# A two-pass planner, one load sequence with few loads on ScalarE, and equal units in a fused delta-rule and MLP kernel

## The chip, the cores and the metric

One core of a Trainium2 chip. The metric is the device time of one execution in microseconds, median over the runs of a kernel. Executions of this kernel have a faster and a slower state: runs over 1.5% above the fastest of the same kernel are called slow and are left out of ratios. Chips differ too: the same kernel before has a median of 415.7 us on the first chip and of 421.6 to 423.4 us on four others, so kernels are compared through the runs of the kernel before on the same chip.

## The reference, cut to what matters

```python
# attention part: batch 4, 8 heads, 768 steps, head size 48
k_n = k / (norm(k) + 1e-6)
for t in range(S):
    y[t]  = g[t] * (q[t] @ state)
    v_old = state.T @ k_n[t]
    state = state + beta[t] * outer(k_n[t], v[t] - v_old)
# then, on the 3072 x 384 result
h = x @ w_in                                        # 384 -> 2048
a = where(h >= 1, h, where(h <= -1, 0, (h + 1)**2 / 4))
out = a @ w_out                                     # 2048 -> 384
```

## The kernel before

The recurrence is cut into 24 steps of 32 tokens, all 32 (batch, head) pairs at once. The work is a list of tasks; a planner (a small simulation that runs while the kernel is built) decides the order of each engine, and the instructions are emitted in that order. In the first profile each engine's computing instructions stand in that order, line by line: all 9,792 matmuls of TensorE, and all computing instructions of ScalarE, VectorE and GpSimd.

Per step, TensorE has the chain kp, up, su (64, 32 and 64 small matmuls) and as fillers the gram group of a later step (64) and the output y (96). For every group of 4 steps there is an inverse of 32x32 triangular blocks, which costs 2 times 128 small matmuls and a serial run of small VectorE or GpSimd instructions. Each small matmul has its own weight load (the first profile counts 9,792 matmuls and 9,792 weight loads in all).

```python
def f_su():                                   # state update, 64 matmuls of 32x32 by 48
    for par in range(2):
        for j in range(J):
            for h4 in range(4):
                nc.tensor.matmul(sps[32*h4:32*h4+32, par, D*j:D*j+D], kq..., u16..., ...)
...
def pe_dur(n): return n * 0.0076              # the plan's time of n small matmuls
```

The MLP works on units of 2 or 4 steps. An "in" task is one PSUM bank of `x @ w_in` (three matmuls of 512 columns, or six of 256), then ScalarE, ScalarE or GpSimd, and VectorE form the activation `gt`; four "out" tasks of four matmuls make 128 rows of the output.

```python
UNITS = [2, 2, 4, 4, 4, 4, 2, 2]
TAIL = 20.0                                   # us of large products left for the end
```

Loads of q, k, v, g come in pieces of 48 KB. Whichever of the sync engine and ScalarE the plan finds free first issues them:

```python
if eng == "SP" and kind == "load":
    alt = [("ACT", dur, lambda ...: nc.scalar.dma_start(out=tile_, in_=src))]
```

Of the kernel before, what the change touches and what calls it, by code (L numbers as in the profile page):

```python
# [10 lines left out]
ALU = mybir.AluOpType  # L11
# [44 lines left out]
class Task:  # L56
    __slots__ = ("opts", "D", "reads", "writes", "deps", "left", "users", "ready", "start", "end", "eng", "fn", "kind", "name", "n", "after", "after_cost", "elems")
# [8 lines left out]
class Plan:  # L66
# [28 lines left out]
    def run(self, nbank, pol):  # L95
        engs = ["PE", "ACT", "DVE", "POOL", "SP"]
        free = {e: 0.0 for e in engs}
        cand = {e: [] for e in engs}
        banks = [[0.0, None] for _ in range(nbank)]
        dma_free = 0.0  # L100
        order = []

        def release(t):
            for e, d, f in t.opts:
                cand[e].append(t)

        for t in self.tasks:
            if t.left == 0:
                release(t)

        def bank_for(t, at):
            for v in t.writes:
                if v.psum and v.bank is None:
                    if pol.psum_full(v.psum):
                        return INF
                    b = min((b[0] for b in banks if b[1] is None), default=INF)
                    return b
            return 0.0

        def dur_of(t, e):  # L120
            for x, d, f in t.opts:
                if x == e:
                    return d, f

        def pick(e):
            c = cand[e]
            if not c:
                return None
            t0 = max(free[e], min(t.ready for t in c))
            if e == "PE":  # L130
                return pol.pick(c, free[e], bank_for)
            hot = [t for t in c if t.kind == "chain"]
            best = None
            late = lambda t: t.kind == "load" and e == "ACT" and t.D > -35.5
            av = sorted((t for t in c if t.ready <= t0 + 1e-9), key=lambda t: (t.kind != "chain", late(t), t.D, t.n))
            for t in av:
                d, _ = dur_of(t, e)
                if t.kind != "chain" and any(h.ready > t0 and t0 + d > h.ready + 0.25 for h in hot):
                    continue
                return t, t0  # L140
            nxt = min((t.ready for t in c if t.ready > t0 + 1e-9), default=None)
            if nxt is None:
                return None
            h = min((t for t in c if t.ready > t0 + 1e-9), key=lambda t: t.ready)
            return h, h.ready

        left = len(self.tasks)
        while left:
            best = None
            for e in engs:  # L150
                p = pick(e)
                if p is not None and (best is None or p[1] < best[1] - 1e-9):
                    best = (p[0], p[1], e)
            if best is None:
                raise RuntimeError("the plan is stuck: " + str([(e, [t.name for t in cand[e]][:8]) for e in engs]) + str([(t.name, [d.name for d in t.deps if d.start is None][:4]) for t in self.tasks if t.start is None and t.left][:12]))
            t, s, e = best
            d, fn = dur_of(t, e)
            if e == "PE":
                d = d + pol.switch(t)
            t.start, t.eng, t.fn = s, e, fn  # L160
            free[e] = s + d
            t.end = s + d
            if t.kind in ("load", "store"):
                dma_free = max(dma_free, s + d + 0.8) + t.after_cost
                t.end = dma_free + 1.2
            for x, _, _ in t.opts:
                cand[x].remove(t)
            for v in t.writes:
                if v.psum and v.bank is None:
                    i = min((i for i in range(nbank) if banks[i][1] is None), key=lambda i: banks[i][0])  # L170
                    v.bank = i
                    banks[i][1] = v
                    pol.psum_take(v.psum)
            for v in list(t.reads) + list(t.writes):
                if v.psum and v.bank is not None and banks[v.bank][1] is v:
                    if all(x.start is not None for x in v.r) and all(x.start is not None for x in v.w):
                        banks[v.bank] = [max(x.end for x in v.r) + LAT, None]
                        pol.psum_give(v.psum)
            pol.done(t)
            order.append(t)  # L180
            left -= 1
            for u in t.users:
                u.left -= 1
                lat = LAT if e != u.opts[0][0] else 0.0
                u.ready = max(u.ready, t.end + lat)
                if u.left == 0:
                    release(u)
        self.span = max(t.end for t in self.tasks)
        return sorted(order, key=lambda t: (t.start, t.n))


class Policy:


    def __init__(self, nstep, units, tail):
        self.nstep, self.tail = nstep, tail
        self.step = 0
        self.inphase = False
        self.mode = None
        self.mlp_left = 0.0  # L200
        self.quota = 0.0
        self.cnt = {"c": 0, "m": 0, "o": 0}
        self.last_mlp = None
        self.lim = {"c": 3, "m": 3, "o": 1}
        self.step_of_mlp = 0
# [16 lines left out]
    def pick(self, c, free, bank_for):  # L222
        def rdy(t):
            return max(t.ready, bank_for(t, free), free)
        chain = [t for t in c if t.kind == "chain"]
# [41 lines left out]
    def done(self, t):  # L267
        if t.eng != "PE":
            return
        if t.kind == "chain":  # L270
# [4 lines left out]
        elif t.kind in ("in", "out"):  # L275
# [4 lines left out]
            if t.kind == "in":  # L280
                for u in t.elems:
                    u.D = self.step + 0.3
# [3 lines left out]
def kernel(  # L286
# [98 lines left out]
    def load_task(D, tile_, src, names, cost, val, eng="SP", dur=0.46, kind="load"):  # L385
        def fn(tile_=tile_, src=src):
            ENG[eng].dma_start(out=tile_, in_=src)
        alt = []
        if eng == "SP" and kind == "load":
            alt = [("ACT", dur, lambda tile_=tile_, src=src: nc.scalar.dma_start(out=tile_, in_=src))]  # L390
        t = P.add(eng, dur, D, fn, [], [val], kind, names, alt=alt)
# [3 lines left out]
    vin = {}  # L395

    def loads(p):
        gi = p // 2
        for nm, src, R, D0 in (("k", k, R_k, 4 * gi - 14), ("q", q, R_q, 4 * gi - 13.9), ("v", v, R_v, 4 * gi - 9), ("g", g, R_g, 4 * gi - 7)):
            val, t = R.new(f"{nm}{p}")  # L400
            vin[nm, p] = (val, t)
            for c in range(2):
                s = 2 * p + c
                for h4 in range(4):
                    a = bass.AP(tensor=src.tensor, offset=src.offset + h4 * S * D + s * C * D, ap=[[D, C], [HS, J], [1, D]])
                    if gi == 0:
                        DD = -40 + {("k", 0): 0, ("k", 1): 1, ("q", 0): 2, ("q", 1): 3, ("v", 0): 4, ("v", 1): 5, ("g", 0): 6, ("g", 1): 7}[nm, p]
                    else:
                        DD = D0 + (p % 2) * 1.0
                    load_task(DD, t[32 * h4:32 * h4 + 32, c], a, f"ld{nm}{p}", 0.285, val)  # L410

    vbeta = Val("beta")
    for st in range(4):
        for h4 in range(4):
            a = bass.AP(tensor=beta.tensor, offset=beta.offset + h4 * S + st * C, ap=[[4 * S, J], [GS * C, NG], [1, C]])
            load_task(-37, braw[32 * h4 + 8 * st:32 * h4 + 8 * st + 8], a, "ldb", 0.05, vbeta, "POOL", 0.45)
# [37 lines left out]
    def prep_pair(p):  # L454
# [7 lines left out]
        P.add("ACT", acost(768), D0, lambda: act("ACT", sqt[:], flat(kt_), AF.Square), [kv], [sq], "", f"ksq{p}")  # L462
# [10 lines left out]
              [kv, v3, nv, vz_kq[a.slot]], [vk, a], "", f"kh{p}")  # L473
# [264 lines left out]


    def w_in_task(a, half, r0, ap_rows):  # L740
        src = bass.AP(tensor=moe_w_in.tensor, offset=moe_w_in.offset + r0[0] * DFF + half * 1024, ap=ap_rows + [[1, 1024]])
        dst = win[r0[1]:r0[1] + r0[2], a, half * 1024:half * 1024 + 1024]
        load_task(-26.6 + 0.05 * half, dst, src, f"win{a}", 1.5 * r0[2] / 128, vwin[half], "POOL", 0.6)

    for half in range(2):
        w_in_task(0, half, (0, 0, 128), [[D * DFF, 4], [DFF, 32]])
        w_in_task(2, half, (4 * D + 16, 0, 128), [[D * DFF, 4], [DFF, 32]])
        for h4 in range(4):
            w_in_task(1, half, (h4 * D + 32, 32 * h4, 32), [[160 * DFF, 2], [DFF, 16]])
    for qd in range(4):  # L750
        src = bass.AP(tensor=moe_w_out.tensor, offset=moe_w_out.offset + qd * 4 * 128 * DM, ap=[[DM, 128], [128 * DM, 4], [1, DM]])
        load_task(-21 + 0.1 * qd, wout[:, 4 * qd:4 * qd + 4, :], src, "wout", 2.2, vwout, "POOL", 0.7)


    for p in range(NSTEP // 2):
        loads(p)
    for gi in range(NG):
# [14 lines left out]
    pol.mlp_left = sum(t.opts[0][1] for t in P.tasks if t.kind in ("in", "out"))  # L772
    order = P.run(NB, pol)
# [7 lines left out]
UNITS = [2, 2, 4, 4, 4, 4, 2, 2]  # L781
TAIL = 20.0
DEBUG = []
# [28 lines left out]
```

## Time and profile before

| | us |
|---|---|
| median, first chip | 415.7 |
| profiled execution (slow) | 424.8 |
| its first su (state update of step 0) | 68.5 |
| its last su (step 22) | 375.1 |
| its last matmul | 412.9 |

How to read it: three regions, cut at those instants. The start fills the buffers and makes the inverse of group 0; the middle is the recurrence with the MLP between; the tail is MLP alone, then the last stores. The profile's lines are shown in the prediction. PE is TensorE, DVE VectorE, ACT ScalarE, POOL GpSimd, SP the sync engine; a trailing q marks an engine's DMA issues. A bracket at the end of a line is how long the engine stood idle before it, and what ended that.

### The profile page before, as it was taken

The page shows a single profiled execution, that of the slowest core. Times are in us where ns is not written, and L with a number is a line of the kernel's source. Part 1 is how long each engine was busy: PE and PEld are TensorE (multiplying, and loading weights), DVE is VectorE, ACT ScalarE, POOL GpSimd, SP SyncE. Part 2 cuts the span into 40 slices and gives each one's busy share as a digit, 9 for nine tenths or more (in the row PEclk, how much of TensorE's full clock was granted, in tenths as well). Part 3 has the DMA queues.
Part 4 walks back from the last instruction along what each step waited for, and adds up shares of the span by engine and source line. Part 5 has one row for each costly group of instructions (what it writes and reads, how often), then busy time and mean ns, then how long its engine had stood idle before and what let it go on. Part 6 is the DMA issues. An engine that isn't in the chain of part 4 may idle for free.

```text
span 424.8 us, 21311 instructions
## 1 busy us (share of the span) xinstructions
PE 261.1 (61%) x9792; PEld 167.7 (39%) x9792; DVE 170.4 (40%) x318; ACT 167.5 (39%) x301; POOL 140.3 (33%) x261
## 2 busy tenths in 40 slices
PE   0030014577876644367578669689867888989980
PEld 0030014455654324334344434445443553546750
DVE  2230824334784225234553535335423313555500
ACT  0500004143782123036353435256544424768920
POOL 8681001035496341045513563058400001011100
PEclk9999999995995665568685759579886986999996
DMA  7899976432334245443313224014011100001101
GB/s 128 130 128 175 149 143 115 75 66 45 66 56 83 62 94 101 95 72 50 60 27 65 46 43 94 5 31 106 13 31 40 42 22 22 22 5 39 39 30 44
DMA packets 114793, 28.23 MB, mean 66 GB/s; under 512 B 108688, under 2 KB 113936, under 8 KB 114704
## 3 DMA queue, kind: packets, MB, share of 16 engines
q1 hardware_dynamic: 77600, 18.16, 22.2%
q10 hardware_dynamic: 30192, 5.46, 7.5%
q0 software_dynamic: 6912, 3.26, 5.5%
q8 instruction: 76, 1.25, 1.2%
q14 instruction: 13, 0.11, 0.1%
HBM read 25.26 MB, written 4.72 MB: 71 GB/s over the span
## 4 chain that ended last, share of the span: by engine, by line
PE 54%; DMA 19%; issue 17%; DVE 3%; POOL 2%; ACT 2%; SPq 1%; ACTq 1%
PE bank L699 18%; PE bank L725 16%; DMA rk<-in_k_dram 5%; DMA rg<-in_g_dram 5%; PE sps L638 4%; DMA rq<-in_q_dram 4%; DMA rv<-in_v_dram 3%; PE bank L654 3%; PE bank L494 3%; PE bank L611 3%; PE bank L627 2%; DMA out_dram<-ot 2%; PE bank L575 2%; PE bank L660 2%; PE bank L562 1%
## 5 line engine op out<-in xcount | busy, mean ns | idle before, releaser
L699 PE MATMUL bank<-xt,win 128*128 128x512 f16 (+1 forms) x384 | 94.1, 381 | 5.9 <-issue 4.7
L725 PE MATMUL bank<-wout,gt 128*128 128x384 f16 x384 | 87.5, 366 | 0.6 <-DVE gt L708 0.6
L708 DVE SCALAR_TENSOR_TENSOR gt<-bank,r 128x512 f16<-128x512 f32 x96 | 63.4, 681 | 47.1 <-ACT r L373 32.6
L373 ACT ACTIVATE rl<-bank 128x512 f32<-128x512 f32 x96 | 56.4, 596 | 58.3 <-PE bank L699 55.7
L705 POOL TENSOR_TENSOR r<-rl 128x512 f32<-128x512 f32 x25 | 26.0, 1041 | 116.6 <-ACT rl L373 96.1
L725 PEld LDWEIGHTS <-gt 128*128 128x128 f16 x384 | 38.9, 107 | 34.1 <-issue 14.9
L699 PEld LDWEIGHTS <-win 128*128 128x128 f16 x384 | 39.2, 109 | 32.0 <-issue 15.6
L472 POOL TENSOR_TENSOR kq<-rk,nn 128x768 f16<-128x768 f32 x12 | 17.7, 1478 | 85.0 <-DMA rv<-in_v_dram 38.2
L494 PE MATMUL bank<-kt 24*32 24x64 f16 x1536 | 22.3, 217 | 37.5 <-DVE nn L467 21.5
L373 ACT ACTIVATE r<-rl 128x512 f32<-128x512 f32 x71 | 43.9, 629 | 1.6
L665 DVE TENSOR_TENSOR y<-bank,rg 128x384 f16<-128x384 f32 x24 | 13.3, 556 | 67.6 <-PE bank L660 48.6
L494 PEld LDWEIGHTS <-kt 24*32 24x32 f16 x1536 | 19.0, 109 | 41.0 <-DVE nn L467 21.5
L616 DVE TENSOR_TENSOR rr<-rv,bank 128x384 f16<-128x384 f32 x23 | 12.7, 552 | 44.7 <-PE bank L611 44.6
L562 PE MATMUL bank<-d,ab 16*32 16x16 f16 x768 | 7.8, 173 | 34.8 <-DVE d L552 25.7
L638 PE MATMUL sps<-u,kq 32*32 32x48 f16 x1472 | 18.6, 194 | 16.5 <-ACT u L373 8.6
L373 ACT ACTIVATE u<-bank 128x384 f16<-128x384 f32 x24 | 11.8, 490 | 42.5 <-PE bank L627 34.6
L373 ACT ACTIVATE s<-sps 128x768 f16<-128x768 f32 x23 | 18.6, 809 | 20.2 <-PE sps L638 19.8
L535 POOL TENSOR_TENSOR xx<-xx,tm 128x28 f32<-128x28 f32 (+6 forms) x70 | 24.3, 347 | 5.2
L654 PE MATMUL bank<-s,kt 24*32 24x48 f16 x1472 | 19.4, 198 | 10.3 <-issue 10.3
L638 PEld LDWEIGHTS <-kq 32*32 32x32 f16 x1472 | 15.4, 98 | 25.5 <-issue 24.8
L532 POOL TENSOR_TENSOR tm<-xx 128x28 f32<-128x28 f32 (+6 forms) x70 | 23.5, 335 | 4.9
L373 ACT ACTIVATE ab<-bank 128x256 f16<-128x256 f32 x24 | 9.1, 382 | 39.6 <-DMA rg<-in_g_dram 15.0
(54 smaller groups left out, 288.7 us busy)
## 6 DMA issues: line engine op xcount, KB each, us to landing
out_dram<-ot SPq DMA_DIRECT2D x24, 192.0 KB, 1.8
rg<-in_g_dram SPq DMA_DIRECT2D x71, 48.0 KB, 2.7
rq<-in_q_dram SPq DMA_DIRECT2D x69, 48.0 KB, 2.6
rk<-in_k_dram SPq DMA_DIRECT2D x67, 48.0 KB, 3.0
rv<-in_v_dram SPq DMA_DIRECT2D x66, 48.0 KB, 2.7
wout<-in_moe_w_out_dram POOLq DMA_DIRECT2D x4, 384.0 KB, 11.1
rv<-in_v_dram ACTq DMA_DIRECT2D x30, 48.0 KB, 2.4
rk<-in_k_dram ACTq DMA_DIRECT2D x29, 48.0 KB, 2.8
```

The source lines that it names most:

```text
L373: nc.scalar.activation(out=out, in_=in_, func=func, **kw)
L472: P.add("POOL", 1.5, D0 + 0.3, lambda: nc.gpsimd.tensor_tensor(out=kqf[:, :, 0, 0:D], in0=flat(kt_), in1=_ap(nt, [[1, 2 * J], [0, D]], 3 * ...
L494: nc.tensor.matmul(b[32 * h4:32 * h4 + 32, 64 * j:64 * j + 64], _apr(kt, 32 * h4, 24, [[2, 32]], j * 128 + par), _apr(kt, 32 * h4, 24, [[2 ...
L532: P.add(sub, d, D0 + 0.1 * jj, lambda jj=jj, n=n, tm=tm: seng.tensor_tensor(out=_ap(tm, [[n * jj, 2], [jj, n], [1, jj]]), in0=_ap(x, [[256 ...
L535: P.add(sub, d, D0 + 0.1 * jj, lambda jj=jj, n=n, tm=tm: seng.tensor_tensor(out=_ap(x, [[256, 2], [16, n], [1, jj]], (jj + 1) * 16), in0=_ ...
L638: nc.tensor.matmul(sps[32 * h4:32 * h4 + 32, par, D * j:D * j + D], _apr(kqt, 32 * h4, 32, [[2, 32]], (c * J + j) * 128 + par), u16[32 * h ...
L654: nc.tensor.matmul(b[32 * h4:32 * h4 + 32, D * j:D * j + D], _apr(kt, 32 * h4, 24, [[2, 32]], j * 128 + 64 + par), s16[32 * h4:32 * h4 + 2 ...
L665: P.add("DVE", dcost(384), s + 0.5, lambda: nc.vector.tensor_tensor(out=y16[:], in0=_ap(bk(yp), [[D, J], [1, D]]), in1=gt_[:, c], op=ALU.m ...
L699: nc.tensor.matmul(b[:, x * nt:x * nt + nt], win[:, kt_, m * 128:m * 128 + 128], xt[:, kt_ * nt:kt_ * nt + nt], start=(kt_ == 0), stop=(kt ...
L705: t2 = P.add("POOL", pcost(512), 0, lambda: nc.gpsimd.tensor_tensor(out=r2[:], in0=rl[:], in1=rl[:], op=ALU.mult), [rv], [r2v], "elem", f" ...
L708: t3 = P.add("DVE", dcost(512), 0, lambda: nc.vector.scalar_tensor_tensor(out=gt[:], in0=bk(hp)[:], scalar=1.0, in1=r2[:], op0=ALU.max, op ...
L725: nc.tensor.matmul(b[:, 0:DM], gt[:, o:o + 128], wout[:, m, :], start=(m == 0), stop=(m == NM - 1))
```

## The change

Its intent: plan TensorE's order first as if the other engines were free, then plan all engines with deadlines that follow from TensorE's times; fix one sequence of loads, with only twelve of them on ScalarE; hold the weights back until the first groups are loaded; make all MLP units two steps long. The core of the diff:

```diff
-        if eng == "SP" and kind == "load":
-            alt = [("ACT", dur, lambda ...: nc.scalar.dma_start(out=tile_, in_=src))]
-        t = P.add(eng, dur, D, fn, [], [val], kind, names, alt=alt)
+        t = P.add(eng, dur, D, fn, [], [val], kind, names)
...
+    FIRST = "k0 k1 q0 q1 k2 q2 k3 q3 v0 v1 g0 g1 v2 k4 q4 k5 q5 v3 g2 g3".split()
+                    on_act = (nm == "k" and p < 2 or nm == "q" and p < 1) and h4 % 2 == 1
+                    eng = "ACT" if on_act else "POOL" if nm + str(p) in POOL_LOADS else "SP"
...  # beta: 16 loads become 4 loads and two VectorE transposes
...  # squares and scaling of k0, k1 may also run on VectorE
+            t = P.add("POOL", 0.65, D, fn, [vin[gate][0]], vals, "load", f"win{a}")   # waits for v0 or v1
+            t = P.add("POOL", 0.7, ..., fo, [vin["v", 3][0]], [vwout], "load", "wout")
...
-    order = P.run(NB, pol)
+    order = P.plan(NB, pol, PASSES)
+    def plan(self, nbank, pol, passes):
+        order = self.run(nbank, pol, ("ACT", "DVE", "POOL"))     # these engines free
+        for i in range(passes):
+            self.deadlines(SLOW)
+            pol.order = {t: n for n, t in enumerate(x for x in order if x.eng == "PE")}
+            order = self.run(nbank, pol)                          # the best pass is kept
...
-UNITS = [2, 2, 4, 4, 4, 4, 2, 2]
+UNITS = [2] * 12
```

## The prediction

> **What bounds the kernel now.** I read the page first (busy shares, slices, chain), then windows cut at the chain's own steps, the list of waits of TensorE, and TensorE's timeline. The page:
>
> ```profile
> PE 261.1 (61%) x9792; PEld 167.7 (39%) x9792; DVE 170.4 (40%) x318; ACT 167.5 (39%) x301; POOL 140.3 (33%) x261
> PE   0030014577876644367578669689867888989980
> PEclk9999999995995665568685759579886986999996
> DMA  7899976432334245443313224014011100001101
> PE 54%; DMA 19%; issue 17%; DVE 3%; POOL 2%; ACT 2%; SPq 1%; ACTq 1%
> ```
>
> TensorE, the busiest engine, is almost unused in the first six of 40 slices (64 us), while DMA is at its fullest; the chain of waits is 54% TensorE, and 17% "issue", waiting for nothing that the profile shows. So there are three regions: a start, the recurrence, a tail. I cut them at the first state update (su of step 0, 68.5 us), the last (375.1) and the last matmul (412.9):
>
> ```profile
> core 0: us, PE busy (x) PEld busy (x) DVE busy (x) ACT busy (x) POOL busy (x), PEclk, DMA share, GB/s
> 0.00:68.50 68.50, 6.88 (x548) 6.15 (x551) 23.98 (x65) 10.23 (x17) 28.91 (x48) 1.00 0.92 142
> 68.50:375.10 306.60, 218.92 (x8681) 137.11 (x8684) 130.25 (x229) 131.30 (x240) 106.22 (x208) 0.77 0.28 55
> 375.10:412.90 37.80, 35.28 (x575) 24.45 (x574) 16.14 (x25) 25.44 (x44) 5.20 (x5) 1.00 0.08 29
> ```
>
> The start: on ScalarE's timeline
>
> ```profile
> 21.63 5.01 ACTq L390 DMA_DIRECT2D rg<-in_g_dram  x4
> 36.49 0.38 ACT L373 ACTIVATE ab<-bank 128x256 f16<-128x256 f32 x1 [9.42 <-DMA rg<-in_g_dram]
> 58.07 5.72 ACTq L390 DMA_DIRECT2D rv<-in_v_dram  x8
> 63.97 0.84 ACT L373 ACTIVATE ksq<-rk 128x768 f32<-128x768 f32 x1 [20.79 <-DMA rv<-in_v_dram]
> 64.72 0.58 ACT L373 ACTIVATE p<-bank 128x512 f16<-128x512 f32 x1
> ```
>
> ScalarE stands behind its own load issues. The gram matmuls of group 0 were done by 30.4 us, but the last eviction `ab` ran at 43; the first matmul of the inverse ran at 56.1 to 57.3, but its eviction `p` at 64.7. About 12 and 7 us of the start are ScalarE blocked by loads that are needed much later.
>
> The recurrence: TensorE's timeline from 160 us
>
> ```profile
> 166.96 0.54 PE L638 MATMUL sps<-u,kq 32*32 32x48 f16 x35 [0.31 <-issue]
> 167.30 1.06 PE L494 MATMUL bank<-kt 24*32 24x64 f16 x64
> 168.14 0.50 PE L654 MATMUL bank<-s,kt 24*32 24x48 f16 x29
> 170.97 0.54 PE L654 MATMUL bank<-s,kt 24*32 24x48 f16 x35 [2.33 <-issue]
> 171.30 0.52 PE L660 MATMUL bank<-u,ms 32*32 32x48 f16 x32
> 171.62 0.69 PE L562 MATMUL bank<-d,ab 16*32 16x16 f16 x61
> 174.97 0.68 PE L562 MATMUL bank<-d,ab 16*32 16x16 f16 x67 [2.65 <-issue]
> ```
>
> The engine stops in the middle of groups that need no semaphore there. From stop to stop it is 35+64+29 = 128 matmuls, with their weight loads 256 instructions; the same holds for nearly all stops of the trace, and never less than about 3.73 us pass between two of them 256 apart. The queue kind "instruction" has 76 packets of 16 KB, and 19,594 instructions are 76.5 times 256. So TensorE is fed by instruction blocks, and one block costs at least 3.73 us. Waits of TensorE on other engines in this region sum to under 20 us: I call it bound by TensorE, by instruction blocks where matmuls are small, by the clock where they are large.
>
> The large matmuls (input product, L699) are very unevenly spread:
>
> ```profile
> 95.70:132.80 37.10, 10.86 (x72) 7.40 (x72) 0.79 0.34 60
> 132.80:187.30 54.50, 4.11 (x9) 1.01 (x9) 0.56 0.44 84
> 187.30:245.20 57.90, 17.27 (x46) 4.64 (x45) 0.74 0.30 52
> 375.10:424.80 49.70, 14.60 (x103) 9.81 (x102) 0.93 0.09 33
> ```
>
> 72 of 384 run while step 4 waits for group 1, 9 in steps 4 to 7, 103 after the last update. With 120 of the 384 output matmuls, 29% of the feed-forward part is left over for the tail.
>
> [...]
>
> **The change, part by part.**
>
> *Loads in one sequence, few on ScalarE.* ScalarE keeps 12 loads (half of k0, k1, q0). In the trace one tensor of one pair (8 loads, 384 KB) takes about 2.7 us in the chain (2.52 to 3.19). So k0, k1, q0, q1 are in by about 14 us, as now. From there with the durations of the trace: ksq 0.84, reduce 0.95, root, add and reciprocal 0.6, kq 1.5, two transposes of 0.7, two gram groups 1.9: about 7 us for each pair, pair 1 by 20 us (now 30.4). Then `ab` 0.4, and from the first transpose `at` to the `d` and `zz` transposes the trace has 43.2 to 56.9, 13.7 us. Then 1.2 + 0.6 + 1.2 + 0.7 for the two inverse products and evictions, up and u 1.0. That sums to 39; with waits between engines I take 42 for the first su instead of 68.5: minus 26.5. Beta comes in 4 transfers instead of 16 (571 ns each on GpSimd: about 7 us of GpSimd less), but 24 loads of k2, v0, v1 and the weights go to GpSimd; at 0.64 us they take 15 us, beside the inverse of group 0 on VectorE.
>
> *Weights wait for v0, v1 and v3.* At 142 GB/s the first two pairs (3.1 MB) take 22 us undisturbed; now the weights start at 13.5 us among them. The weights then land by about 45 and 75 us, an estimate; the first input product is possible when y0 and y1 are done, about 55 us. This costs nothing if the output product has enough else ahead of it.
>
> *Units of 2 throughout.* Sixteen products of 3 matmuls over 512 columns become eight of 6 over 256, in four units, each twice: 384 input matmuls become 576. With weight loads 384 instructions more, 1.5 blocks, at most 6 us. Columns are the same: the page of groups and the timeline have 0.65 us for six of 256 as for three of 512 at full clock. The gain is that input products become ready every 2 steps, so steps 4 to 7 are not left without.
>
> *Planner.* It has no model of instruction blocks or of the half clock, so it can't aim at either. It should spread large matmuls by quota and leave 20 us of them for the tail.
>
> *Sum, in the profiled run's time.* The middle now: 17,365 instructions, 67.8 blocks, in 306.6 us: 4.52 us each. The stretches differ: 187 to 245 us, 3,959 instructions at 3.74 us a block, at the floor; 245 to 315 us, 3,434 at 5.2, because the feed-forward part is concentrated there at clock 0.79. Evenly mixed, a block has about 1.25 us of small matmuls and 2.6 products of 0.65 us, 2.95 in all at full clock (so the floor of 3.73 counts), and about 4.9 at half clock. Half and half gives 4.3. Blocks: 67.8 plus 1.3 for added instructions plus 0.5 for products moved out of the tail: 69.6 times 4.3 is 299 us. The tail now takes 49.7 with 223 large matmuls; with about 155 I take 40. So 42 + 299 + 40 = 381. The profiled run before had 424.8 against a median of 415.89, factor 0.979: 373 us.
>
> **The rivals.** (1) *The block floor eats the middle.* If blocks stay at 4.5 us, the earlier start just moves the same middle forward: 42 + 313 + 40 = 395, times 0.979, 387 us. For it: the planner does not know the floor, and it groups small matmuls between quotas. Against: the stretch at 3.74 with some large products. (2) *The opposite:* [...]the blocks at 3.9: 42 + 271 + 37 = 350, 343 us. [...] (3) *Late loads take ScalarE's place:* with loads on the sync engine alone (about 0.6 us each to issue, 4.8 us a tensor against 2.7 us of transfer) and 6.3 MB of weights later, an in-order TensorE may stand behind a product whose weights have not landed. That would give back 10 to 20 us around 50 to 90 us: 385 to 393. For it: the sync queue already waits 124 us for `ot` before stores. Against: DMA is 28% busy in the middle. (4) *No gain,* the fixed order stalling on durations that the plan has wrong: about 415. It would need new waits of 40 us, and there are under 20 of all now.
>
> **Range and chances.** The start is the surest term (20 to 30 us), the block time the least (3.95 to 4.6, so 275 to 320 us for the middle). I say 373 us, 350 to 394 eight times in ten; faster by over 2% 0.92, within 2% 0.06, slower 0.02.
>
> **What would show it.** First su near 42 us and no ScalarE wait on its own loads; first large matmul by 55 to 60 us; stops still 256 instructions apart and 3.73 us at least; large matmuls in every step, about 155 after the last su; TensorE's loads and matmuls 9,984 each. I am wrong if su of step 0 comes after 55 us, if TensorE's waits for DMA or weights grow by tens of us, or if the middle stays near 4.5 us a block.

The second rival's 3.9 us a block (350, 343 us in all) is left as the author's estimate, not shown by a trace.

What the first profile shows for the terms. Every clock record in it is 0.50 or 1.00. Matmuls of an input product begin 213 ns apart at 0.50 and 109 at 1.00 with 256 columns, 426 and 216 ns with 512 (medians), so a product takes 1.28 us at 0.50 and 0.65 at 1.00. A group of 64 small matmuls over 48 columns takes 0.65 us at 0.50 (from 187.3 us) and 0.49 at 1.00 (from 261.2). With these, 1.25 us of small matmuls at full clock and 2.6 products come to about 5.0 us at 0.50, near the 4.9 of the prediction.

## The result, and the profile after

Ratios here and below are the mean time of one kernel's fast runs over that of the kernel before in the same rounds, so not quite the ratio of the medians.

| | before | after |
|---|---|---|
| median, us | 415.67 | 394.83 |
| ratio, 95% interval | 1 | 0.9471 (0.9385 to 0.9557) |

The kernel is faster, by about half of what was predicted. The median lies 0.8 us beyond the upper end of the predicted range; the ratio times 415.67 us gives 393.7, just inside it. The page after the change, the lines that answer to those of before:

```profile
PE 266.9 (68%) x9984; PEld 191.3 (49%) x9984; DVE 176.7 (45%) x324; ACT 165.5 (42%) x298; POOL 143.3 (36%) x268
PE   0122347955654779798698579767967769988970
PE 61%; issue 18%; DMA 7%; DVE 5%; ACT 4%; SPq 3%; ACTq 0%; DVEq 0%
```

TensorE works from slice 2 on and its low slices are fewer. On the chain, DMA has gone from 19% to 7%; "issue" is still there with 18%.

The first profile of before was taken in the slow state, the profile after in the fast one. So the kernel before was profiled again (run before_again below, 418.51 us, a single run and so of unknown state, but at the level of the fast runs of before on that chip, which is not the first chip). Windows cut at first su, last su, last matmul and end, before:

```profile
0.00:66.70 66.70, 6.87 (x544) 6.13 (x545) 23.93 (x65) 10.23 (x17) 28.89 (x48) 1.00 0.93 146
66.70:367.30 300.60, 213.73 (x8674) 134.96 (x8673) 130.37 (x229) 130.99 (x240) 106.15 (x208) 0.80 0.29 56
367.30:404.90 37.60, 35.35 (x575) 24.50 (x574) 16.15 (x25) 25.50 (x44) 5.20 (x5) 1.00 0.08 29
```

and after, the same cuts:

```profile
0.00:52.60 52.60, 10.83 (x804) 9.64 (x804) 36.02 (x82) 11.41 (x22) 36.65 (x71) 1.00 0.79 134
52.60:353.60 301.00, 230.60 (x8686) 163.74 (x8688) 128.11 (x222) 137.70 (x247) 100.41 (x192) 0.80 0.35 67
353.60:380.80 27.20, 25.48 (x503) 17.92 (x502) 12.62 (x20) 15.88 (x28) 6.28 (x7) 0.94 0.08 24
```

The columns are the window, its length, busy time and count of TensorE's matmuls, its weight loads, VectorE, ScalarE and GpSimd, the granted clock, DMA share and GB/s. Of the 23.9 us between the two executions the start gives 14.1, the tail 10.4; the middle is as long as before, 300.6 against 301.0 us. The two profiles are from different chips (on one chip the medians differ by 20.8 us), and on a third chip the changed kernel had a middle of 307.1 us (after_again below), so this split is good to some 6 us.

The cut at the first su hides one thing. Step 4 cannot begin before group 1 is ready; its su comes at 131.4 us before and at 101.0 after, 30.4 us earlier. But of the 192 large tasks ("in" and "out") only 14 instead of 27 are done between the first su and that of step 4, and 147 instead of 117 from there to the last su. That last stretch takes 252.6 us instead of 235.9: much of what the early steps gain is work put off.

The clock column needs care: a time without any clock record is counted as 1.00, and the traces have no record before 93.1 us (before, first profile) and 74.2 us (after). In the trace after, a matmul of `x @ w_in` takes 421 ns (median) from 62.9 to 73.9 us, without a record, the same as from 93.8 to 127.9, where the recorded clock is 0.50, and 273 ns from 129.0 to 136.9, where it is 1.00. So the 1.00 of the start windows does not show a full clock.

ScalarE no longer stands behind loads at the start:

```profile
21.91 0.38 ACT L454 ACTIVATE ab<-bank 128x256 f16<-128x256 f32 x1 [0.78 <-PE bank L587]
46.96 0.60 ACT L454 ACTIVATE p<-bank 128x512 f16<-128x512 f32 x1 [6.33 <-PE bank L655]
```

Both evictions now wait for TensorE alone: the last `ab` of group 0 at 21.9 us (43 before), `p` at 46.96, 0.1 us after the end of its matmuls. What TensorE does there is new:

```profile
40.10 0.92 PE L655 MATMUL bank<-d,ab 16*32 16x16 f16 x95
46.47 0.39 PE L655 MATMUL bank<-d,ab 16*32 16x16 f16 x33 [5.45 <-issue]
47.61 0.92 PE L668 MATMUL bank<-zz,p 32*32 32x16 f16 x95 [0.74 <-ACT p L454]
50.20 0.39 PE L668 MATMUL bank<-zz,p 32*32 32x16 f16 x33 [1.67 <-issue]
```

The inverse's matmuls stop twice in mid-group for nothing but "issue", 7.1 us together. The middle has the same stops as before:

```profile
174.76 0.37 PE L720 MATMUL bank<-rr,zz 32*32 32x48 f16 x30 [0.67 <-issue]
175.06 0.82 PE L818 MATMUL bank<-wout,gt 128*128 128x384 f16 x4
175.81 0.67 PE L731 MATMUL sps<-u,kq 32*32 32x48 f16 x64
176.30 0.43 PE L747 MATMUL bank<-s,kt 24*32 24x48 f16 x30
178.76 0.40 PE L747 MATMUL bank<-s,kt 24*32 24x48 f16 x34 [2.03 <-issue]
```

From stop to stop 30+4+64+30 = 128 matmuls, 256 instructions with the weight loads, in 4.00 us, two of them standing.

### The profile page after: what moved, and what is told of

The parts are those of the page before. It is cut to its first block, busy times and chain, and to the rows that moved or that the text cites. A ratio compares the mean times of both kernels' runs of the same rounds, so it can differ in the third digit from the quotient of the medians.

```text
span 392.9 us, 21772 instructions
## 1 busy us (share of the span) xinstructions
PE 266.9 (68%) x9984; PEld 191.3 (49%) x9984; DVE 176.7 (45%) x324; ACT 165.5 (42%) x298; POOL 143.3 (36%) x268
## 3 DMA queue, kind: packets, MB, share of 16 engines
q0 software_dynamic: 6208, 4.44, 7.1%
q8 instruction: 78, 1.28, 1.3%
## 4 chain that ended last, share of the span: by engine, by line
PE 61%; issue 18%; DMA 7%; DVE 5%; ACT 4%; SPq 3%; ACTq 0%; DVEq 0%
PE bank L792 21%; PE bank L818 17%; PE sps L731 4%; PE bank L587 4%; PE bank L747 4%; PE bank L704 4%; DMA rk<-in_k_dram 3%; SPq L468 3%; PE bank L720 2%; DMA rq<-in_q_dram 2%; PE bank L753 2%; PE bank L655 2%; DMA out_dram<-ot 2%; DVE xx L628 1%; PE bank L668 1%
## 5 line engine op out<-in xcount | busy, mean ns | idle before, releaser
L792 PE MATMUL bank<-xt,win 128*128 128x256 f16 x576 | 96.6, 320 | 2.5 <-issue 1.9
L798 POOL TENSOR_TENSOR r<-rl 128x512 f32<-128x512 f32 x27 | 27.9, 1039 | 172.9 <-ACT rl L454 144.9
L818 PE MATMUL bank<-wout,gt 128*128 128x384 f16 x384 | 89.4, 371 | 0.0
L801 DVE SCALAR_TENSOR_TENSOR gt<-bank,r 128x512 f16<-128x512 f32 x96 | 64.5, 683 | 49.6 <-ACT r L454 24.7
L792 PEld LDWEIGHTS <-win 128*128 128x128 f16 x576 | 62.3, 113 | 25.1 <-issue 7.2
L587 PE MATMUL bank<-kt 24*32 24x64 f16 x1536 | 22.3, 222 | 43.1 <-DVE kt L577 32.3
L454 ACT ACTIVATE r<-rl 128x512 f32<-128x512 f32 x69 | 43.1, 629 | 2.6 <-POOL tm L625 0.4
L753 PE MATMUL bank<-u,ms 32*32 32x48 f16 x768 | 12.5, 196 | 18.7 <-issue 18.7
L731 PE MATMUL sps<-u,kq 32*32 32x48 f16 x1472 | 17.5, 194 | 11.1 <-ACT u L454 9.3
L731 PEld LDWEIGHTS <-kq 32*32 32x32 f16 x1472 | 15.2, 98 | 17.6 <-issue 17.3
L454 ACT ACTIVATE s<-sps 128x768 f16<-128x768 f32 x23 | 18.6, 808 | 10.9 <-PE sps L731 10.6
L454 ACT ACTIVATE ot<-bank 128x384 f32<-128x384 f32 x24 | 11.7, 488 | 23.8 <-PE bank L818 18.5
```

Source lines behind the costliest of these rows:

```text
L454: nc.scalar.activation(out=out, in_=in_, func=func, **kw)
L587: nc.tensor.matmul(b[32 * h4:32 * h4 + 32, 64 * j:64 * j + 64], _apr(kt, 32 * h4, 24, [[2, 32]], j * 128 + par), _apr(kt, 32 * h4, 24, [[2 ...
L731: nc.tensor.matmul(sps[32 * h4:32 * h4 + 32, par, D * j:D * j + D], _apr(kqt, 32 * h4, 32, [[2, 32]], (c * J + j) * 128 + par), u16[32 * h ...
L753: nc.tensor.matmul(b[32 * h4:32 * h4 + 32, D * j:D * j + D], ms[32 * h4:32 * h4 + 32, j, :], u16[32 * h4:32 * h4 + 32, j, :], start=(s == ...
L792: nc.tensor.matmul(b[:, x * nt:x * nt + nt], win[:, kt_, m * 128:m * 128 + 128], xt[:, kt_ * nt:kt_ * nt + nt], start=(kt_ == 0), stop=(kt ...
L798: t2 = P.add("POOL", pcost(512), 0, lambda: nc.gpsimd.tensor_tensor(out=r2[:], in0=rl[:], in1=rl[:], op=ALU.mult), [rv], [r2v], "elem", f" ...
```

## The experiments

Two theories at first. **Theory A:** TensorE is fed in blocks of 256 instructions that take at least 3.7 us each (in the first profile 76 packets of 16 KB of the kind "instruction" for 76.5 times 256 instructions, and mostly 3.73 to 4.0 us between two "issue" stops that far apart), so the middle is bound by the number of instructions; the start was bound by ScalarE behind its loads. **Rivals:** TensorE's busy time or its clock, the chain through the other engines, the order of the loads, or the planner itself.

### Where the gain comes from

A caution for all runs but gram_twice and in_twice: after each edit the planner orders everything anew, so besides the named condition the order changes too. Differences of one or two per cent can come from that; no run here separates the two.

**before_again**, the kernel before, unchanged.

> The kernel before, unchanged, to have its profile in the fast state (the first one, 424.8 us, was slow against a median of 415.7). Theory A (the prediction's): the slow state stretches all regions alike, so first su near 67, su to su about 300, tail about 48.5. Rival B: the middle alone is longer in the slow state; then a fast middle of about 295 us means that the change did not shorten the middle at all (301 us after it).

Measured: 418.51 us; 66.7 + 300.6 + 37.6 + 11.9 us, the windows shown above. A holds but for the tail: it expected 67, 300 and 48.5 us (the last two parts together are 49.5). The start is 0.974 of that in the slow profile, the middle 0.980, the tail with the stores 0.996. B's fast middle of 295 us is not reached, but most of the difference in microseconds, 6.0 of 8.0, lies in the middle, which is its largest part. The two executions also ran on different chips, so state and chip are not separated. Against the slow profile the change seems to shorten the middle by 5.6 us; against this one it does not.

**before_units2**, the units alone:

```diff
-UNITS = [2, 2, 4, 4, 4, 4, 2, 2]
+UNITS = [2] * 12
```

> The kernel before with twelve units of two steps, nothing else of the change. Theory A: the units spread the input products, so the tail shrinks from 49 to about 40 us and the middle gains a few us by mixing, minus up to 6 us for 1.5 instruction blocks: 403 to 410 us. Rival B: the planner spreads badly in any case, and the added blocks cost: 414 to 422 us.

Measured: 411.48 us, ratio 0.976 (0.9698 to 0.9822, so it stays open whether the gain reaches 2%), first su at 68.5. Between the two, nearer to A: the part after the last su until the last matmul falls from 37.6 to 30.5 us, because 80 output matmuls are left there instead of 120; the middle is 299.1 us for 1.8 blocks more.

**old_planner**, everything of the change except the planner: the classes `Plan` and `Policy` of before, with `order = P.run(NB, pol)`.

> The loads, beta path, VectorE alternatives and units of the change under the old one-pass planner. Theory A: the start is due to the loads alone, so first su by 50 to 54 us as in the changed kernel and 395 to 402 us in all. Rival B: the two passes are what makes the start or the middle shorter; then 408 to 420 us.

Measured: 397.65 us, ratio 0.9426 (0.9371 to 0.9481). The total is A's, the first su is not: 61.8 us. So A's reason is incomplete. What counts for the second pass: with it (0.9471 and 0.9452) the kernel is not faster than without (0.9426). The new planner moves the first su 9 us forward and loses that in the middle, which is 293.1 us here (on another chip than 301.0).

**after_units_old**, the changed kernel with the old units.

> The changed kernel with the old units (2, 2, 4, 4, 4, 4, 2, 2). Theory A: the units are worth the 10 us of the tail: 402 to 408 us, first su still at 52 to 53 us, over 200 large matmuls after the last su. Rival B: the new planner spreads these as well, 1.5 blocks fewer: 388 to 394 us.

Measured: 394.54 us, ratio 0.9329 (0.9244 to 0.9414). A falls, B holds (393.5 us for the fast runs alone). Under the old planner the units brought 2.4%; under the new one they bring nothing that can be shown, and the interval allows that they cost a little.

**before_sp_loads**, the kernel before with one condition changed:

```diff
-        if eng == "SP" and kind == "load":
+        if False:
             alt = [("ACT", dur, lambda ...: nc.scalar.dma_start(out=tile_, in_=src))]
```

> The kernel before with the one change that ScalarE may issue no load, so that all q, k, v, g loads go through the sync engine. Theory A (ScalarE standing behind its own load issues made the start long): first su at 50 to 56 us instead of 67, total 6 to 14 us less than before, ratio 0.965 to 0.985. Rival B (the order of the loads and the weights among them set the start): first su stays above 62 us and the ratio at 0.99 to 1.01.

Measured: 403.9 us, ratio 0.9565 (0.9502 to 0.9629), first su at 51.5 us. A holds, and the gain is over the upper end of its range: this one condition brings 4.35% of the 5.3 to 5.5% of the whole change. ScalarE's eviction `p`:

```profile
44.36 0.60 ACT L373 ACTIVATE p<-bank 128x512 f16<-128x512 f32 x1 [15.41 <-PE bank L562]
```

The stretch from the su of step 4 to the last su, before_again first, then before_sp_loads:

```profile
131.40:367.30 235.90, 168.08 (x6762) 101.11 (x6750) 96.70 (x167) 100.84 (x182) 76.22 (x150) 0.77 0.26 53
129.20:351.10 221.90, 161.83 (x6794) 99.56 (x6797) 97.16 (x168) 102.14 (x183) 72.98 (x144) 0.78 0.32 62
```

`p` runs 1.3 us after its matmuls began at 43.1, instead of 8.6 us after (56.1 and 64.7 in the first profile). The first su comes 15.2 us earlier, the middle is 299.6 us (300.6 before) and the span 14.9 us shorter. That looks like the same middle begun earlier, but it is not: the su of step 4 comes at 129.2 us, only 2.2 us earlier (it needs the inverse of group 1), and the other steps to the last su take 14.0 us less. So the condition is shown to be worth 4.35%, and the start to be shorter by it; that the end moves because the start did is not shown. One piece of the later gain can be seen: TensorE's waits for ScalarE's `u` after step 4 fall from 9.3 to 2.4 us; the longest before (5.6 us, at 157.0) came when ScalarE had stood 7.6 us for a load of k. The rest was not traced.

**weights_free**, the changed kernel with weight loads that wait for nothing:

```diff
-            t = P.add("POOL", 0.65, D, fn, [vin[gate][0]], vals, "load", f"win{a}")
+            t = P.add("POOL", 0.65, D, fn, [], vals, "load", f"win{a}")
```

and the same for w_out.

> The changed kernel with its weight loads waiting for no q, k, v, g load. Theory A (this part carries little, the start is bound by the VectorE inverse and the blocks): first su at 51 to 56 us, ratio 0.935 to 0.955, no difference. Rival B (the weights take bandwidth from the first groups): first su later than 57 us and 4 to 10 us more in all.

Measured: 404.43 us, ratio 0.9539 (0.9468 to 0.9611), first su at 53.8. A for the first su and, by the centre of the interval, for the total (control after_again: 0.9452, 0.9372 to 0.9531). The two intervals overlap, so whether the gate is worth 0.9% or nothing stays open. The first su is not the place to look for B: the su of step 4 comes at 117.8 us, 14.3 later than in the control (103.5), with the grams of steps 6 and 7 only at 103 to 106 us. Without the gate group 1 is late, and most of that is made up later. That is what B would look like at the second group; the run does not show whether bandwidth or the new order caused it.

### What bounds the middle

**after_again**, the control for the next two.

> The changed kernel, unchanged, on the chip of the next runs, as their control: about 0.947 of the kernel before, first su at 52 to 53 us, no difference between the theories.

Measured: 399.62 us, ratio 0.9452; first su at 52.0 us. As expected.

**gram_twice**: each gram group is issued twice, with the same result.

```diff
-            for par in range(2):
+            for par in (0, 1, 0, 1):
                 for j in range(J):
```

> Every gram group of 64 small matmuls is issued twice into the same bank with the same result; the plan and the order stay the same. Added: 1,536 matmuls and as many weight loads, 12 blocks of 256 instructions, and about 16 us of array time at full clock (24 times 0.65). Theory A (instruction blocks bound the middle): 30 to 45 us more than the changed kernel. Rival B (TensorE's busy time or the clock bounds it): 12 to 20 us more. Rival C (the chain through VectorE and ScalarE bounds it): under 8 us more.

**in_twice**: two of the eight input products of a unit are issued twice, with the same result.

```diff
-            for x in range(per):
+            for x in list(range(per)) * (2 if i < 2 else 1):
```

> Two of the eight input products of each unit are issued twice, 144 large matmuls more, the same result and order. Added: as much array time as in gram_twice (15.6 us at full clock, up to 31 at half) but only 288 instructions, 1.1 blocks. Theory A: [...]0 to 10 us more, far less than gram_twice. Rival B: the same as gram_twice or more, 12 to 30 us. Rival C: under 8 us.

The 31 us at half clock follow from the first profile: a product takes 1.28 us at a recorded clock of 0.50 and 0.65 at 1.00.

Measured, means of the fast runs: control 398.5 us, gram_twice 442.3, in_twice 410.5. So 43.8 us for 12 blocks and 16 us of array time, and 11.9 us for 1.1 blocks and 15.6 us of array time. The middles, control first:

```profile
52.00:359.10 307.10, 234.27 (x8686) 164.67 (x8686) 128.16 (x222) 137.82 (x247) 100.69 (x193) 0.78 0.35 66
```

gram_twice:

```profile
70.20:405.60 335.40, 242.44 (x9706) 175.49 (x9705) 128.56 (x222) 137.79 (x247) 100.17 (x191) 0.78 0.30 57
```

in_twice:

```profile
53.40:367.20 313.80, 236.37 (x8817) 172.59 (x8817) 127.92 (x222) 137.42 (x247) 100.16 (x191) 0.84 0.34 64
```

In gram_twice the middle grows by 28.3 us, while TensorE's busy time in it grows by 8.2: the rest is standing. Its 1,020 matmuls more are 8.0 blocks, 3.5 us each. The start grows by 18.2 us for the other four blocks, so what was meant as a test of the middle found 4.5 us a block in the start. Over the whole kernel 43.8 us by 12 blocks is 3.65 us each. That is near the block floor of A, and neither busy time nor the chain (rival C: under 8 us) explains it. In_twice lies just beyond A's range and at the lower edge of B's: large products are cheap beside small ones, 11.9 us against 43.8 for the same array time, but not free. The reading that fits both runs is a middle with two limits that take turns: blocks where matmuls are small, array time where they are large. The second half of it is not shown by itself: in in_twice the recorded clock of the middle also rose, from 0.78 to 0.84, and its busy time grew by only 2.1 us. In the changed kernel the large products of the middle are busy for 161.3 us (85.9 input, 75.4 output); at full clock, where the trace has 0.65 us for one task of either kind, their 83 input and 78 output tasks would take 105 us.

**blocks1**: the changed kernel with a planner that knows the blocks. The simulated TensorE starts a new block at the earliest 3.73 us after the one before it, and:

```diff
+            if rb <= free + 0.1 and self.stall(t, r) > STALL:     # a small group would stand
+                return tb, rb                                     # a large product goes first
+FETCH = 3.73
+STALL = 0.8
```

Durations are set to the trace's (small matmul 10.2 ns, product 0.75 us, load of 48 KB 0.33 us).

> The changed kernel with a planner that knows the instruction blocks: each block of 256 TensorE instructions starts at least 3.73 us after the one before it, and where the next group of small matmuls would stand for its block by over 0.8 us, a large product goes first. Durations are set to those of the trace (small matmuls 10.2 ns, a product 0.75 us, a 48 KB load 0.33 us). Theory A (blocks bound the middle, and large matmuls run in their shadow): issue waits of TensorE in the middle fall from about 69 to under 45 us, and the kernel takes 365 to 385 us on this chip, ratio 0.865 to 0.915. Rival B (the clock takes back what the mix gives, or stops come at other places): 390 to 402 us, ratio 0.93 to 0.95.

What the first profile shows of A's "shadow": from 277.3 to 300.4 us 1,280 instructions, large products among them, go by with a stop only at the last of the five steps of 256.

**blocks_off**: the same with `STALL = 1e9`, so no large product is put first.

> The same planner with the same durations and the same block rule in its clock, but without the preference (no large product is put first for a block). Theory A: the preference is what counts, so 388 to 402 us, about the changed kernel. Rival B: it is the better durations that help; then as fast as blocks1 within 2%.

Measured: blocks1 393.08 us, blocks_off 402.44, before 422.83. One run of blocks1 had 385.62 us, and by that the other three (392.72 to 393.76) count as slow, so there is no ratio of fast runs. The one fast run is 17.6 us below the mean of the fast runs of blocks_off (403.2), the other three about 10; by the medians blocks1 is 7.0% below before and 2.3% below blocks_off. So the preference helps, by somewhere between a third and two thirds of what A expected (some 27 us to the centre of its range), and the new durations alone do not (0.9544, against 0.9452 and 0.9471 for the changed kernel). A's range of 365 to 385 us is missed, by 0.6 us in the best run and by 8 in the median. "Issue" waits of TensorE in the whole trace sum to 64.8 us (73.9 without the preference, 67.1 in the changed kernel); in the middle alone they are 56, where A expected under 45. Most stops remain. By its median blocks1 is the lowest relative to before, together with the changed kernel on the old units (0.9329); the two were not run on one chip and can't be ordered.

### What the start is worth

In the changed kernel the inverse of group 0 on VectorE, from its first transpose to its last, took from 22.3 to 41.7 us, 19.4 us, where the kernel before took 13.7. VectorE did the preparation of pairs 2 and 3 in between, and two of the inverse's short instructions took 1.5 us instead of 0.26, each beside a GpSimd instruction (the scaling `kq`, 1.47 us, at 27.06 and 34.58):

```profile
27.14 1.52 DVE L625 TENSOR_TENSOR tm<-xx 128x100 f32<-128x100 f32 x1
```

This one takes 1.52 us where the next of the kind takes 0.27, and it ends 0.1 us after the GpSimd instruction. Other VectorE instructions beside a `kq` are not longer in this trace: the `gt` at 202.26 and 253.40 us take 0.69 us, as elsewhere. Why these two are is not shown.

**start_first**: the inverse of group 0 ahead of all other VectorE work, and the grams of steps 6 and 7 after the inverse's matmuls.

```diff
-            return (t.A, t.n)
+            return (t.name not in FIRST_INVERSE, t.A, t.n)
...
+        if s in LATE_GRAMS:            # (6, 7)
+            tg.after = (mm2_of[0],)
```

> The changed kernel with VectorE's inverse of group 0 ahead of all other VectorE work, and the grams of steps 6 and 7 after the two inverse matmuls. Theory A (the start lost its 10 us to interruptions of the inverse, 19.4 us instead of 13.7, and to stops for instruction blocks behind the early grams): first su at 43 to 47 us instead of 52 to 52.6, and the whole kernel 4 to 8 us shorter, ratio 0.925 to 0.938. Rival B (the blocks of the start come late whatever the order, because loads are in the way): first su stays above 49 us. Rival C (the first su moves, the end does not, because step 4 waits for group 1, which is now later): first su below 48 us, step 4 still at 101 to 104 us, ratio 0.94 to 0.95.

Measured: 398.2 us, ratio 0.9371 (0.9323 to 0.9419), first su at 43.9 us. TensorE:

```profile
43.85 0.82 PE L734 MATMUL sps<-u,kq 32*32 32x48 f16 x63 [0.59 <-ACT u L454]
45.80 1.89 PE L588 MATMUL bank<-kt 24*32 24x64 f16 x127
58.58 0.83 PE L734 MATMUL sps<-u,kq 32*32 32x48 f16 x64 [0.58 <-ACT u L454]
```

The first su comes 8.1 us earlier than in the control, the second at 58.6 us against 58.4: the gram groups of steps 4 to 7, 256 matmuls or two blocks, now stand between the two. Step 4 is at 102.9 (control 103.5). The steps are as C expected. The ratio lies just inside A's range, but its interval reaches into C's and overlaps the control's (0.9372 to 0.9531), so the total does not decide. The early first su, bought by moving blocks behind it, brought no gain that can be told from the control.

## Why the prediction was right or wrong

*The direction and the kinds of gain: right.* Start and tail shrink, the stops stay 256 instructions apart and 3.4 to 4 us at least where matmuls are small, and ScalarE issues no load after the first ten microseconds. (Already in the first profile one pair of stops is 3.45 us apart, not 3.73.) The counts of matmuls and of large ones left after the last su (78 + 72 = 150, about 155 predicted) are right. TensorE's waits for other engines did not grow. Of the signs that it named, the first large matmul came at 62.9 us, not by 55 to 60, and the middle stayed at 4.43 us a block, near the 4.5 that was to show it wrong.

*The start: mechanism right, the term "42" mis-sized; it measured 52.6.* Its first half held: the last `ab` at 21.9 us, against 20.4. Then 13.7 us for VectorE's inverse was taken from a trace in which VectorE had little else to do; it measured 19.4. And the inverse's matmuls and evictions were summed from busy times, without the block floor that the same prediction had just read: they stopped for 7.1 us. Under both lies, as far as these runs show, one cause: the plan put the grams of steps 4 to 7, with their VectorE preparation, in front. Start_first shows that they cost about the same wherever they stand. before_sp_loads shows what the shortening came from: taking the load issues off ScalarE is enough for 15.2 us of it.

*The middle: the failed step is the block time.* Mixing was to lower it from 4.52 to 4.3 us. In the profiles before_again and after it is 4.44 before (17,347 instructions in 300.6 us) and 4.43 after (17,374 in 301.0). That the term, 69.6 blocks or 299 us, lies near the measured 301.0 is luck: it was in the time of a slow run, whose middle was 306.6. The large products did mix in, 161 tasks instead of 144, or 11 us more of them at full clock (105 against 94), with no loss of time: TensorE's stops for "issue" in the middle fall from 68.1 to 58.4 us and its other waits from 18.6 to 12.5, while its busy time grows from 213.7 to 230.6. That is the tail's gain, and the only one of the mixing. The term's own working was also off: 2.6 products a block do not fit the 155 large matmuls that it left for the tail, which make it 2.3; and its 29% of the feed-forward part left over counts matmuls of two sizes, in tasks it is 48 of 192, 25%. Rival 1, blocks staying at 4.5 us, was the nearest to what happened.

*The tail: right.* 39.3 us, 40 predicted.

*The factor 0.979: not a failed step.* before_again has the start at 0.974 and the middle at 0.980 of the slow profile, and only the tail at 0.996. So scaled, the three terms are 41, 293 and 39 us; measured were 52.6, 301.0 and 39.3. The missing 20 us are 11.5 of the start and 8.3 of the middle.

*A reading of the first trace that does not hold, and a pair of runs.* The 1.00 beside the start has no clock record behind it (see the result). Nor do the 142 GB/s of that start show that issuing from two engines pays. The pair to compare is before_again, where the sync engine and ScalarE issue these loads and the time up to the first su moves 146 GB/s (66.7 us), and before_sp_loads, with the sync engine alone, where it moves 127 (51.5 us) and the kernel is 4.35% shorter.

*The share of each part.* The title part of the change, two passes, shows no gain (0.9426 without it, 0.9471 and 0.9452 with it). Most of it can be had by ScalarE issuing no loads (0.9565 alone), partly in the start and partly after step 4. A reason that fits, though not tested by itself, is that the plan has no notion of blocks: it can't trade what it doesn't count. Giving it that notion brought another 2.3% against the same planner without the preference, far less than the 60 to 70 us of stops; what keeps the rest is open.

## What to carry to other kernels

In the kernel before, ScalarE computed and issued loads, and stood with its next computation behind loads that it had issued (9.42 us before an `ab`, 20.79 before a `ksq`); look for brackets that name a DMA in front of an instruction that reads none of its data. Where TensorE stops in mid-group at a fixed count of instructions (256 here), count instructions, not matmul time (43.8 us for 12 blocks added, 11.9 for 1.1 with the same array time): work moved from one place to another keeps its blocks, as the four gram groups did in start_first, and an earlier milestone is a gain only if no work was moved behind it: look at a second milestone too, as step 4 here, before you credit the first. Take a baseline's regions from a profile in the same state as the one that you will compare with, before you subtract.

## What else the traces show of the stops

- With small matmuls a block costs, in the first profile, mostly 3.73 to 4.0 us from one "issue" stop to the next 256 instructions later (3.45 at the least); there are 60 to 75 us of stops in most of these kernels, and 43.8 us for 12 blocks added (3.65 us each).
- A slow stretch did not spare the next stop: in the kernel before, first profile, only 1,280 instructions went by in the 23 us up to 300.4, and TensorE stopped again 512 instructions later, at 313.8 us, for 2.41 us.
- Most stops in the middle last up to about 3 us; longer ones stand where much is loaded: 5.45 us at the start of the changed kernel (161 GB/s from 40.0 to 46.5 us), 4.46 at its 125.0 us (102 GB/s from 118). In gram_twice the longest is 5.3 us. That loads cause it was not tested.
